# An attention and gated-MLP kernel on one core: blocks 3 to 8 in pairs with seven products of sums, and all work behind the first block in one written order

## The chip, the cores and the metric

The kernel runs on one core of one Trainium2 chip. The metric is device time of one execution in microseconds, the median of several runs. The engines are named as in the profile: PE (TensorE; PEld is its weight load), DVE (VectorE), ACT (ScalarE), POOL (GpSimd), SP (SyncE, which here only issues DMA).

## The reference

Attention of q over keys and values that were averaged over groups of eight positions (B, H, S, D = 8, 8, 576, 64), then an RMS norm and a gated MLP over all 4608 tokens (512 to 1536 to 512), all in float32:

```python
k_p = k.reshape(B, H, Sp, 8, D).mean(axis=3); v_p = ...      # 72 pooled keys
attn = softmax(scale * q @ k_p^T)                              # over 72 keys
x = (attn @ v_p)                     # to (4608, 512)
xn = x / sqrt(mean(x * x) + 1e-6) * rms_g
g, val = xn @ w_gate, xn @ w_val
out = (g * sigmoid(g) * val) @ w_out
```

The MLP weights come as float64 words.

## The kernel before, in words

Every float32 operand of a large matrix product is split into a high part (rounded to fp32r) and a low part (the rest); a product is the sum of three matmuls, high by high, low by high, high by low. Tokens are worked in nine blocks of 512 (`NB`), numbered 0 to 8; the attention is worked in eight batches of 576 tokens, so a block takes tokens from one or two batches. The hidden size of 1536 is cut into 12 pieces f of 128 gate and 128 value columns, written 0 to b in the orders.

For a block i and a piece f: `mm1(i, f, 0)` and `mm1(i, f, 1)` (12 matmuls each over four chunks c of 128 inputs, line 490) fill one PSUM bank with the gate and one with the value; `gate` (ACT, Silu, L497) and `val` (DVE, L502) make the activation; `act_hi` (ACT, L506) and `act_lo` (DVE, L510) split it; `mm2` (L521) adds 12 matmuls into four PSUM banks that hold the block's output until the last f, when it is copied and stored (L527, L528).

The attention of a batch goes by four pairs of heads: pooled keys and values (DVE, L228, L239), scores (`s_heads`, PE, L282), softmax with maximum, subtraction, exponent, sum, and the scaling on POOL (L291 to L299), a transpose on DVE and twelve small DMA copies that place the blocks (`s_turn`, L304, L309), the product with the values (`s_av`, PE, L343), copies, squares (ACT) and their sum (POOL, L384). After four pairs `s_sums` and `s_rms` give the norm's factor: PE sums over partitions (L399), ACT takes the root, DVE the reciprocal (L402), and DVE scales the tokens (L404).

Block 0, the attention of batches 0 and 1 and the conversion of the weights follow an order written out by hand (`ORDER`, one letter a step). The rest is laid out by loops: for each block the split of its tokens (`split_x`, L462, L463), then for each f the two halves of the first layer, the second layer of the f before, and between them, by slots, the attention steps of later batches. Each engine runs its instructions in the order in which they stand.

## Time and profile before

| | |
|---|---|
| median of 3 runs | 1048.86 us (1048.38 to 1048.91) |
| the profiled execution | 1049.04 us, its span 1047.3 us |
| PE busy | 1026.6 us, 98% of the span |
| DVE, ACT, POOL busy | 506.3, 416.6, 115.9 us |
| DMA | 65.44 MB, mean 62 GB/s |

The span runs from the first to the last instruction. Busy times are those of one engine alone, so they overlap. A group of instructions is one line of the program on one engine with one shape: its busy time, the mean of one, then the idle time of the engine just before them and who ended it. The chain that ended last is followed back from the last instruction; it is 88% PE, 5% DVE.

### The profile page before, as it was taken

Reading aid. Unit: us, or ns where it says so; the run is one execution under the profiler, and the core shown is the slowest. Engines: PE = TensorE matmul, PEld = TensorE weight load, DVE = VectorE, ACT = ScalarE, POOL = GpSimd, SP = SyncE. Lnnn points to the kernel's source line nnn. Section 1 sums busy time; section 2 is a strip of 40 time slices with the busy share of each in tenths; the row PEclk is TensorE's granted clock in tenths of the full one; section 3 lists DMA queues with packets and bytes.
Section 4 is the critical chain, followed back from the end, with each engine's and each line's share of the span. In section 5 each row is a group of like instructions: output and inputs, shape, how many; then the busy total and the mean of one; then the engine's idle time right before and its main releaser. Section 6 shows DMA issues by size and latency. Waiting matters only on the chain.

```text
span 1047.3 us, 13134 instructions
## 1 busy us (share of the span) xinstructions
PE 1026.6 (98%) x4994; PEld 816.2 (78%) x4994; DVE 506.3 (48%) x857; ACT 416.6 (40%) x771; POOL 115.9 (11%) x108
## 2 busy tenths in 40 slices
PE   7899998999999999999999999999999999999998
PEld 6677776777877777777877787778777888888886
DVE  6799985635455446344653455445452431122112
ACT  5767664433443345333533354335342431121111
POOL 2313430111001100111001101110011000000000
PEclk8599999999999999999999999999999999999999
DMA  9445412222022201221122103210210010001001
GB/s 292 133 163 177 170 62 72 74 76 74 25 73 73 58 25 50 77 66 36 43 75 54 57 3 108 55 53 12 88 36 14 1 41 1 1 1 41 1 1 40
DMA packets 38702, 65.44 MB, mean 62 GB/s; under 512 B 6384, under 2 KB 20208, under 8 KB 37360
## 3 DMA queue, kind: packets, MB, share of 16 engines
q1 hardware_dynamic: 38640, 64.61, 20.3%
q8 instruction: 39, 0.64, 0.3%
q14 instruction: 23, 0.19, 0.1%
HBM read 47.19 MB, written 9.44 MB: 54 GB/s over the span
## 4 chain that ended last, share of the span: by engine, by line
PE 88%; DVE 5%; DMA 2%; ACT 2%; issue 1%; SPq 0%; ACTq 0%
PE psg L490 53%; PE po L521 27%; PE pss L282 4%; PE psx L343 3%; DVE wt L140 1%; DMA wx<-w 1%; DVE wt L144 1%; DMA main<-kT 1%; DVE wt L136 1%; ACT prob L260 1%; PE psr L412 1%; DVE w L162 0%; PE pst L323 0%; PE psb L436 0%; DMA q<-qT 0%
## 5 line engine op out<-in xcount | busy, mean ns | idle before, releaser
L490 PE MATMUL psg<-xh,w 128*128 128x512 f32 x1728 | 541.3, 395 | 2.9 <-ACT xh L462 2.9
L490 PEld LDWEIGHTS psg<-xh,w 128*128 128x128 f32 x1728 | 322.3, 189 | 82.9 <-ACT xraw L350 3.4
L490 PE MATMUL psg<-xl,w 128*128 128x512 f32 x864 | 338.2, 392 | 0.0
L521 PE MATMUL po<-w,hh 128*128 128x512 f32 x864 | 223.3, 395 | 0.0
L502 DVE TENSOR_TENSOR act<-act,psg 128x512 f32<-128x512 f32 x108 | 73.6, 682 | 288.1 <-PE psg L490 254.5
L521 PEld LDWEIGHTS po<-w,hh 128*128 128x128 f32 x864 | 162.6, 188 | 37.7
L490 PEld LDWEIGHTS psg<-xl,w 128*128 128x128 f32 x864 | 162.6, 188 | 35.5 <-DVE xl L463 0.7
L506 ACT CAST hh<-act 128x512 fp32r<-128x512 f32 x108 | 67.1, 622 | 212.5 <-DVE act L502 212.4
L497 ACT ACTIVATE act<-psg 128x512 f32<-128x512 f32 x108 | 64.5, 597 | 204.8 <-PE psg L490 202.6
L521 PE MATMUL po<-w,hl 128*128 128x512 f32 x432 | 122.4, 395 | 0.4 <-DVE hl L510 0.4
L521 PEld LDWEIGHTS po<-w,hl 128*128 128x128 f32 x432 | 79.5, 188 | 20.3 <-DVE act L502 2.0
L510 DVE TENSOR_TENSOR hl<-act,hh 128x512 fp32r<-128x512 f32 x102 | 70.0, 686 | 40.9 <-ACT hh L506 38.5
L299 POOL TENSOR_TENSOR prob<-prob,sm 128x360 f32<-128x360 f32 x48 | 38.7, 826 | 446.2 <-DVE sm L297 257.9
L497 ACT ACT_TABLE_LOAD x40 | 51.3, 1283 | 47.8 <-PE psg L490 26.6
L291 DVE TENSOR_REDUCE mx<-pss 128x5 f32<-128x360 f32 x48 | 23.4, 528 | 49.8 <-PE pss L282 49.6
L304 DVE STREAM_TRANSPOSE sq<-prob 128x960 f32<-128x960 f32 x24 | 28.3, 1179 | 38.8 <-POOL prob L299 34.6
L384 POOL TENSOR_TENSOR acc<-acc,sq 128x576 f32<-128x576 f32 x21 | 30.7, 1461 | 146.4 <-ACT sq L378 146.4
L239 DVE TENSOR_REDUCE pv<-v 72x128 f32<-72x1024 f32 x28 | 34.0, 1214 | 22.8 <-PE psx L343 21.5
L282 PEld LDWEIGHTS pss<-pk,q 64*128 64x128 f32 x560 | 34.5, 193 | 12.0 <-issue 8.9
L282 PE MATMUL pss<-pk,q 64*128 64x72 f32 x560 | 38.6, 283 | 1.8 <-DVE own L329 0.9
L294 ACT ACTIVATE prob<-prob 128x360 f32<-128x360 f32 x48 | 23.1, 505 | 31.9 <-DVE prob L293 31.8
L343 PE MATMUL psx<-pt,pv 72*64 72x256 f32 (+2 forms) x224 | 35.4, 429 | 0.0
(90 smaller groups left out, 701.2 us busy)
## 6 DMA issues: line engine op xcount, KB each, us to landing
wx<-w SPq DMA_DIRECT2D x10, 1024.0 KB
v<-vN SPq DMA_DIRECT2D x32, 288.0 KB
out<-o SPq DMA_DIRECT2D x36, 256.0 KB
wx<-w SPq DMA_DIRECT2D x16, 512.0 KB
k<-kT SPq DMA_DIRECT2D x28, 288.0 KB
q<-qT SPq DMA_DIRECT2D x28, 288.0 KB
pt<-sq SPq DMA_DIRECT2D x96, 40.0 KB
pt<-sq SPq DMA_DIRECT2D x96, 32.0 KB
```

Of the source, the lines that this page charges most:

```text
L239: nc.vector.tensor_reduce(pv, s["v"], AX.X, ALU.add)
L282: nc.tensor.matmul(s["ps", h][:, t * SP:(t + 1) * SP], s["q"][r, o:o + P], s["pk"][r, :], start=True, stop=True)
L299: nc.gpsimd.tensor_tensor(pr, pr, sm[:, :, None].broadcast_to(shape), ALU.mult)
L304: nc.vector.transpose(sq.rearrange("p b g j -> p g b j"), prob.rearrange("p g (b j) -> p g b j", b=3))
L343: nc.tensor.matmul(ps[r, :n], s["pv"][:, r], s["pt"][:, h, tok], start=True, stop=True)
L384: nc.gpsimd.tensor_add(acc[b], acc[b], st[b, p]["sq"])
L490: nc.tensor.matmul(ps[:, :NB], w[:, c, cols], x[c], start=(j == 0), stop=(j == len(todo) - 1))
L497: nc.scalar.activation(t, ps[:, :NB], AF.Silu)
L502: nc.vector.tensor_mul(t, t, ps[:, :NB])
L506: nc.scalar.copy(a, st["act"])
L510: eng.tensor_sub(l, st["act"], hh[i, f].bitcast(F32))
L521: nc.tensor.matmul(po[i][t], x[i, f][:, t * P:(t + 1) * P], w, start=(f == 0 and k == 0), stop=(f == NF - 1 and k == 2))
```

## The change

The loops behind block 0 are replaced by a second written order, `LATER`, of 2279 steps with names of two letters and digits (batch, pair, head or block, f, product). Each engine again takes its own steps in that order. The tokens of block 1 are split (`t0` to `t3`) ahead of the last second-layer step of block 0 (`ob`).

Blocks 1 and 2 keep the old first layer (`mg`, `me`). Blocks 3 and 4, 5 and 6, 7 and 8 form pairs. For a pair, the tokens of the two blocks and the two halves of the 512 inputs form a 2 by 2 matrix A of parts (A11, A12 of the first block, A21, A22 of the second), gate and value columns and the two halves of the inputs a 2 by 2 matrix B; the four products of the first layer come from seven products of parts and of sums of parts (Strassen's scheme in Winograd's form):

```python
PRODUCTS = (("A11", "B11"), ("S2", "T2"), ("A12", "B21"), ("S3", "T3"), ("A22", "T4"), ("S1", "T1"), ("S4", "B22"))
```

The sums S of tokens are made by DVE (`p_sum`, step `ys`), split by ACT and DVE (`yh`, `yl`). The sums T of weights are made once, during blocks 1 and 2, on POOL (`wt`, `wf`), split by ACT and POOL (`wh`, `wl`) and stored to DRAM (`ws`); the weights' own blocks are stored as well (`wd`). Each product then loads its weights (256 KB) from DRAM into one of eight buffers (`rl`), in order on SP's queue. A product is six matmuls:

```diff
+    def product(i, f, k):
+        if k in (0, 4):
+            st["X"] = bank(2, f"px{i}_{f}_{k}")
+        elif k in (1, 3, 5):
+            st["Y"] = bank(3, f"py{i}_{f}_{k}")
+        ps = st["Y"] if k in (1, 3, 5, 6) else st["X"]
+        w, x = ring[i, f, k], XP[i, PRODUCTS[k][0]]
+        more = k in (2, 6)
+        todo = [(c, h) for c in range(2) for h in ((0, 0), (1, 0), (0, 1))]
+        for j, (c, (a, b)) in enumerate(todo):
+            nc.tensor.matmul(ps[:, :NB], w[:, a, c, :], x[:, b, c, :],
+                             start=j == 0 and not more, stop=j == len(todo) - 1, skip_group_check=more)
```

Between the products DVE and ACT take the sums out of the two banks:

```diff
+            cp=lambda i, f: S_.copy(later(i, f), st["X"]),
+            u2=lambda i, f: V.tensor_add(u2(i), later(i, f), st["Y"]),
+            sa=lambda i, f: S_.activation(new_act(i, f), st["X"], AF.Silu),
+            u3=lambda i, f: V.tensor_add(u3(i), u2(i), st["Y"]),
+            c2=lambda i, f: V.tensor_sub(later(i, f), u3(i), st["X"]),
+            sw=lambda i, f: S_.activation(later(i, f), later(i, f), AF.Silu),
+            v2=lambda i, f: V.tensor_add(u3(i), u3(i), st["Y"]),
+            v1=lambda i, f: V.tensor_add(u2(i), u2(i), st["Y"]),
+            va=lambda i, f: V.tensor_mul(st["act"], st["act"], u2(i)),
+            vb=lambda i, f: V.tensor_mul(later(i, f), later(i, f), u3(i))))
```

The first block's second layer runs in two halves (`mp`) among the products of the next f; the activations of the second block are kept (`later`) and its second layer (`mo`) runs by itself behind the pair, with the outputs of the first block copied (`ev`) and stored (`st`) ahead of it.

The scaling of a batch is now four instructions for each half of its tokens, with the gain in it, so that the split of later blocks has no factor; the scores are laid out so that a copy of the transposed blocks is contiguous:

```diff
-        x = xraw[b][:, :, tok]
-        nc.vector.tensor_mul(x, x, r[:, None, :].broadcast_to([P, NC, n]))
+    def l_scale(b, u):
+        r, tok = half(b, u)
+        for c in range(NC):
+            x = xraw[b][:, c, tok]
+            nc.vector.scalar_tensor_tensor(x, x, gcol[:, c:c + 1], r, ALU.mult, ALU.mult)
...
-                    t[32 * i:32 * i + n, :, o:o + w],
-                    sq[32 * a:32 * a + n, i].rearrange("p (h t) j -> p h (t j)", h=2)[:, :, :w])
+                nc.sync.dma_start(t[32 * i:32 * i + n, o // 16:(o + w) // 16, :],
+                                  sq[32 * a:32 * a + n, i, :w // 16, :])
```

Of the order, the end of block 2 with the start of the first pair, a step of the first pair, the end of that pair, and a step of the last pair (steps of all engines; `mo`, `mp`, `rm`, `sc`, `av`, `pr` are PE's):

```diff
+ mo2a vl2b wf93 wh91 sh4 wl93 hi2b sl4 wl91 lo2b ws93 rm40:0 ws91 rm41:1 rt40 rl300 rl301 rl302
+rl303 rt41 rl304 rc40 rl305 sc51:01 wh94 rl306 wl94 rl310 wh92 lv52 rc41 wl92 ws94 lk52 ws92 wtb rs41 wfb0 rs40 wfb1
+wfb2 wfb3 ys33 yh30 yh32 yl30 whb3 yh33 wlb3 ys34 pr300 yh31 wsb3 rl311 yl33 whb2 yh34 wlb2 ys35 cp30 wsb2 whb1 wlb1
+yl34 yh35 wsb1 yl35 pr301 whb4 wlb4 ys36 rl312 wta wsb4 u230 yh36 yl31 wfa0 wfa1 wha1 yl36 pr302 wfa2 wha3 wla3 yl32
+mp2b0 rl313 sa30 wfa3 wsa3 wla1 pr303
...
+pr310 rl320 v130 va30 sq50 pr311 rl321 cp31 sm510 hi30 ev22 nm510 pr312 rl322 lo30
+st22 ev23 u231 st23 mp300 sa31 rl323 tr51 sc52:01 dm51 pr313 mx521 sb521 mx520 pr314 ex521 u331 sb520 pr315 c231
+ex520 sm521 sw31 mp301 v231 nm521 sm520 pr316 vb31
...
+pr3b6 lk71 vb3b nm701 av630:1 rl510 v13b av631:0 va3b xc630 tr70 hi3b xc631 lo3b
+dm70 xd63 mo3b hi40 pv71 lo40 sq63 pk71 jn63 mo40 hi41 ev30 ev31 ev32 ev33 lo41 sh6 mo41 sl6 hi42 lo42
...
+pr720 rl730
+v171 va71 pr721 rl731 cp72 hi71 pr722 lo71 rl732 u272 mp710 rl733 sa72 pr723 pr724 rl734 u372 pr725 rl735 c272 sw72
+mp711 rl736 v272 vb72 pr726
```

More of the change, by code (lines that the diff above doesn't have):

```diff
@@ L448, in body, with tokens @@
     hh, hl, po = {}, {}, {}
-    def split_x(i):
-        XH[i] = [sb1.tile([P, NB], F32R, tag=f"xh{c}", name=f"xh{i}_{c}") for c in range(NC)]
-        XL[i] = [sb1.tile([P, NB], F32R, tag=f"xl{c}", name=f"xl{i}_{c}") for c in range(NC)]
-        parts, t = [], i * NB
-        while t < (i + 1) * NB:
+    tails = {}
+    def tokens(t, n):
+        parts, end = [], t + n
+        while t < end:
             b, o = divmod(t, S)
-            n = min(S - o, (i + 1) * NB - t)
-            parts.append((xraw[b], o, n, t - i * NB))
+            n = min(S - o, end - t)
+            x, first = tails.get(b, ((xraw[b][:, :2], xraw[b][:, 2:]), 0))
+            parts.append((x, b, o - first, n))
@@ new lines, in place, with w_sum, w_sumhi @@
+    def place(f, name):
+        r, c = {**BLOCKS, **SUMS}[name]
+        return st["whole", f][:, 2 * r:2 * r + 2, c * P:(c + 1) * P]
+    def w_sum(f, k):
+        y, a, b = (("T1", "T3", "T1"), ("T3", "B22", "T3"), ("T2", "B22", "T1"), ("T4", "T2", "B21"))[k]
+        nc.gpsimd.tensor_sub(place(f, y), place(f, a), place(f, b))
+    def w_sumhi(f, k):
+        if f < AHEAD:
+            y = sb2.tile([P, 2, 2, P], F32R, tag="out", name=f"wt{f}_{k}")
+        else:
+            turn = st["turn"] = 1 - st.get("turn", 0)
+            y = room()[:, 1, :].rearrange("p (s h c n) -> p s h c n", s=2, h=2, c=2)[:, turn].bitcast(F32R)
+        st["parts", f, k] = y
+        nc.scalar.copy(y[:, 0], place(f, f"T{k}"))
@@ new lines, in w_sumlo, with w_store, at @@
+    def w_sumlo(f, k):
+        y = st["parts", f, k]
+        nc.gpsimd.tensor_sub(y[:, 1], place(f, f"T{k}"), y[:, 0].bitcast(F32))
+    def w_store(f, k):
+        x = wsums[f, k] = dram.tile([P, 2, 2, P], F32, tag=f"sum{f}_{k}", name=f"sum{f}_{k}")
+        nc.sync.dma_start(x, st["parts", f, k].bitcast(F32))
+    def at(q, k, lo, hi):
+        d = 0
+        for x, _, o, n in q:
+            if d <= lo and hi <= d + n:
+                return x[k][:, :, o + lo - d:o + hi - d]
+            d += n
@@ new lines, in p_pieces, with p_hi @@
+    def p_pieces(i, n):
+        name = XPARTS[n]
+        if name[0] == "S":
+            yield slice(0, NB), XP[name]
+            return
+        q, d = tokens((i + (name[1] == "2")) * NB, NB), 0
+        for _, _, _, m in q:
+            yield slice(d, d + m), at(q, int(name[2]) - 1, d, d + m)
+            d += m
+    def p_hi(i, n):
+        X = XP[i, XPARTS[n]] = space1(n + 1, [P, 2, 2, NB], F32R, f"xp{i}_{n}")
+        for t, x in p_pieces(i, n):
+            nc.scalar.copy(X[:, 0, :, t], x)
@@ new lines, in between, with u2, u3, later @@
+    def between(i):
+        if ("u", i) not in st:
+            st["u", i] = space1(NF - 1, [P, 4 * NB], F32, f"u{i}")
+        return st["u", i]
+    def u2(i):
+        return between(i)[:, :NB]
+    def u3(i):
+        return between(i)[:, NB:2 * NB]
+    def later(i, f):
+        if ("hb", i, f // 4) not in st:
+            st["hb", i, f // 4] = space1((9, 8, 10)[f // 4], [P, 4, NB], F32, f"hb{i}_{f}")
+        return st["hb", i, f // 4][:, f % 4, :]
+    def new_act(i, f):
+        t = st["act"] = sb1.tile([P, NB], F32, tag="act", name=f"act{i}_{f}")
+        return t
@@ L481, in mm1 @@
     def mm1(i, f, which):
-        ps = st["psg", which] = bank(1, f"psg{i}_{f}_{which}")
+        ps = st["psg", which] = bank(2 + which, f"psg{i}_{f}_{which}")
         cols = slice(which * P, (which + 1) * P)
@@ new lines, in o_copy @@
+    def o_copy(i, t):
+        name = f"o{i}_{t}"
+        if i == NBLK - 1:
+            o = sb1.tile([P, DM], F32, tag=f"xh{t}", name=name)
+        elif i >= FIRST and not second(i):
+            if ("o", i) not in st:
+                st["o", i] = space1(0, [P, NB // P, DM], F32, f"o{i}")
+            o = st["o", i][:, t, :]
+        else:
+            o = sb2.tile([P, DM], F32, tag="out", name=name)
+        st["o", i, t] = o
+        (nc.scalar.copy if t % 2 else nc.vector.tensor_copy)(o, po[i][t])
@@ L569, in first_phase, with o_store, run @@
+    def o_store(i, t):
+        nc.sync.dma_start(out[i * NB + t * P:i * NB + (t + 1) * P, :], st["o", i, t])
+    def run(order, n, steps):
+        for step in order.split():
+            step, _, banks = step.partition(":")
+            given[:] = [int(x) for x in banks]
+            steps[step[:n]](*(int(x, 36) for x in step[n:]))
+            assert not given, step
     def first_phase():
@@ L596, in body @@
         first_phase()
[L597 to L631 removed]
+        later_phase()
 def kernel(q, k, v, moe_w_gate, moe_w_val, moe_w_out, moe_rms_g):
```

425 lines of the change are left out of this document (284 added, 141 removed).

## The prediction

> **What bounds the kernel now.** I read the page's busy times, then the windows by stage (columns: stretch, its length, then for PE, PEld, DVE, ACT, POOL busy us and instructions; granted clock, DMA share, GB/s), then the chain.
>
> ```profile
> span 1047.3 us, 13134 instructions
> PE 1026.6 (98%) x4994; PEld 816.2 (78%) x4994; DVE 506.3 (48%) x857; ACT 416.6 (40%) x771; POOL 115.9 (11%) x108
> ```
>
> ```profile
> 0.00:57.00 57.00, 47.82 (x279) 36.33 (x280) 42.33 (x90) 38.72 (x146) 14.52 (x19) 0.67 0.62 195
> 57.00:176.00 119.00, 114.02 (x565) 89.70 (x563) 103.41 (x133) 72.30 (x149) 37.05 (x23) 1.00 0.38 128
> 176.00:184.00 8.00, 5.39 (x15) 3.90 (x16) 5.29 (x11) 4.26 (x10) 0.00 (x0) 0.79 0.72 216
> 184.00:510.00 326.00, 325.82 (x1631) 258.00 (x1630) 160.91 (x290) 132.61 (x203) 33.54 (x35) 1.00 0.20 56
> 510.00:843.00 333.00, 333.00 (x1634) 263.96 (x1634) 153.41 (x276) 133.31 (x207) 30.83 (x31) 1.00 0.16 47
> 400.00:510.80 110.80, 110.80 (x550) 87.77 (x549) 52.97 (x97) 45.31 (x71) 10.78 (x11) 1.00 0.19 54
> 843.00:942.00 99.00, 99.00 (x435) 81.25 (x434) 21.66 (x34) 18.40 (x30) 0.00 (x0) 1.00 0.03 11
> ```
>
> From 184 us on TensorE (PE) is never idle (325.82 of 326, 333.00 of 333), at full clock. So from there the time is the number of matmuls by their pace, and other engines count only where they make PE wait. Block 7 (843 to 942) has no attention beside it and takes 99.0 us; a block with one batch of attention takes 110.8. A batch thus costs PE 11.8 us (2.95 for each of four head pairs), and DVE 52.97 - 21.66 = 31.3. The pace of a matmul, from the chain:
>
> ```profile
> 925.42 5.47 PE psg L490 x24
> 930.89 2.77 PE po L521 x12
> 933.66 5.47 PE psg L490 x24
> ```
>
> 36 matmuls take 933.66 - 925.42 = 8.24 us, 0.229 each. The only loss behind the first block is at the start of block 1, in the timeline of PE:
>
> ```profile
> 175.08 0.63 PE L521 MATMUL po<-w,hh 128*128 128x512 f32 x2
> 178.61 0.73 PE L490 MATMUL psg<-xh,w 128*128 128x512 f32 x2 [2.91 <-ACT xh L462]
> ...
> 180.72 1.06 PE L490 MATMUL psg<-xh,w 128*128 128x512 f32 x2
> 181.58 0.63 PE L490 MATMUL psg<-xl,w 128*128 128x512 f32 x1
> ```
>
> PE idles 2.91 us for the split of block 1, and its matmuls then come every 0.43 us (180.72, 181.58: two each) until 183.5. That is half pace; the window 176 to 184 shows the clock, 0.79 on average.
>
> **Part 1, seven products: what goes.** A pair of blocks computes, for each of the 12 column pairs f, 7 products of 6 matmuls (42) where two blocks took 2 x 24 = 48. The second layer stays at 24. 6 x 12 x 3 pairs = 216 matmuls fewer: 216 x 0.229 = **-49.4 us**. The attention's own matmuls stay, as many as before.
>
> **Part 2, start of block 1.** Its split (t0 to t3) now stands ahead of the last second-layer step of block 0 and is hidden by it. The 2.91 us of idle go, and half of a slow stretch of about 3.4 us: **-4.6**. If that cover failed, these 4.6 would stay.
>
> **Part 3, the products' chain.** Per f PE now runs 42 + 12 matmuls, 12.36 us. DVE has u2, u3, c2, v2, v1, va, vb, lo; ACT has cp, sa, sw, hi. Nearest rows by form and the timeline around one release:
>
> ```profile
> L502 DVE TENSOR_TENSOR act<-act,psg 128x512 f32<-128x512 f32 x108 | 73.6, 682 | 288.1 <-PE psg L490 254.5 <-issue 33.6
> L510 DVE TENSOR_TENSOR hl<-act,hh 128x512 fp32r<-128x512 f32 x102 | 70.0, 686 | 40.9 <-ACT hh L506 38.5 <-PE po L521 2.4
> L506 ACT CAST hh<-act 128x512 fp32r<-128x512 f32 x108 | 67.1, 622 | 212.5 <-DVE act L502 212.4
> L497 ACT ACTIVATE act<-psg 128x512 f32<-128x512 f32 x108 | 64.5, 597 | 204.8 <-PE psg L490 202.6 <-POOL hl L510 1.3 <-DVE hl L510 0.6
> L497 ACT ACT_TABLE_LOAD x40 | 51.3, 1283 | 47.8 <-PE psg L490 26.6 <-DVE hl L510 21.0
> ```
>
> ```profile
> 185.95 0.39 PE L490 MATMUL psg<-xl,w 128*128 128x512 f32 x1
> 186.44 0.69 DVE L502 TENSOR_TENSOR act<-act,psg 128x512 f32<-128x512 f32 x1 [0.45 <-PE psg L490]
> 187.17 0.62 ACT L506 CAST hh<-act 128x512 fp32r<-128x512 f32 x1 [3.04 <-DVE act L502]
> ```
>
> DVE 8 x 0.68 = 5.5 us, ACT 2.4. The last matmul starts at 185.95, so its place ends at 186.18; DVE begins 0.26 later, and the next engine 0.04 after DVE ends. Products write banks X, Y in turn, and a bank read by DVE must be free one group (6 x 0.229 = 1.37 us) later: 0.26 + 0.68 + 0.04 = 0.98. cp needs 0.26 + 0.60 + 0.04 = 0.90; sa with a table load has two groups, 2.74, for 2.2. So a pure pair step makes no wait, with 0.4 us to spare; cover gone, each late 0.5 us costs 0.5. In the first pair DVE has two batches besides (2 x 31.3), the last parts (some 12) and 12 x 5.5: 141 us of PE's 12 x 12.36 + 8 x 2.95 = 172, or 82%, in one fixed order. The attention's instructions:
>
> ```profile
> L291 DVE TENSOR_REDUCE mx<-pss 128x5 f32<-128x360 f32 x48 | 23.4, 528 | 49.8 <-PE pss L282 49.6
> L293 DVE TENSOR_TENSOR prob<-pss,mx 128x360 f32<-128x360 f32 x48 | 23.7, 522 | 0.0
> L296 DVE TENSOR_REDUCE sm<-prob 128x5 f32<-128x360 f32 x48 | 23.0, 521 | 0.3
> L298 DVE RECIPROCAL sm<-sm 128x5 f32<-128x5 f32 x48 | 8.0, 187 | 0.1
> L304 DVE STREAM_TRANSPOSE sq<-prob 128x960 f32<-128x960 f32 x24 | 28.3, 1179 | 38.8 <-POOL prob L299 34.6 <-DMA pt<-sq 4.2
> ```
>
> I followed one full step by hand, f = 1, from the start of pr310: v1 ends at 0.94, va 1.6, sm (0.52 and two small ones) 2.5, an output copy 3.2, lo 3.9, u2 4.6 (its bank is wanted at 7.1), tr 5.8; scores end at 7.1; mx, sb, mx to 8.95, u3 9.6 (wanted 9.84), sb 10.2, c2 10.9, sm 11.8, v2 12.5 (wanted 12.6). It fits by 0.1 us. So the waits lie between nothing and half a us in each of the 24 steps of the two pairs with attention (12); I take **+4**, nearer the low end, as that step fits.
>
> **Part 4, start of the first pair.** Block 4 needs batch 4, whose scaling is the last work of stage two (blocks 1 and 2). PE's order there is mo2a, rm40, rm41, sc51, pr300, pr301, pr302. On DVE stand between rm41 and pr300: rc40, rc41, rs41, rs40 (four instructions each), ys33, yl30. Nearest rows:
>
> ```profile
> L401 ACT ACTIVATE acc<-psr,eps 128x288 f32<-128x288 f32 x12 | 6.0, 500 | 7.9 <-PE psr L399 7.9
> L402 DVE RECIPROCAL acc<-acc 128x288 f32<-128x288 f32 x12 | 23.4, 1952 | 13.1 <-ACT acc L401 13.0
> L463 DVE SCALAR_TENSOR_TENSOR xl<-xraw,gcol,xh 128x320 fp32r<-128x320 f32 x8 | 4.3, 543 | 2.3 <-ACT xh L462 2.3
> L463 DVE SCALAR_TENSOR_TENSOR xl<-xraw,gcol,xh 128x256 fp32r<-128x256 f32 x8 | 3.4, 478 | 2.3 <-ACT xh L462 2.3
> L162 DVE TENSOR_TENSOR w<-wt,w 128x1024 fp32r<-128x1024 f32 x6 | 7.3, 1215 | 0.0
> ```
>
> 288 columns lie between 0.478 and 0.543: 0.51. These two rows leave some 0.2 that no column pays for (0.543 less 320 times 0.065 / 64). A sum over 1024 is 1.2, and 0.15 to 0.2 more for each further piece: ys 1.5 in three pieces, yl of a block 1.4 in two, of a sum 1.25. Root 0.5 + 2 x 1.95 + 8 x 0.51 + 1.5 + 1.4 = 11.4; PE has sc51 alone beside it (half of a head pair's 2.95, 1.5): it waits 9.9. pr301 needs S2: ys34, yl33, ys35, yl34 = 5.5 against one product of 1.37: 4.1. pr302 needs A12, behind yl35, ys36, u230: 4.8 against 1.37: 3.4. **+17.4**. Ends: 12, if the two later waits are mostly hidden by slower products; 25, if rm40 comes late as well, behind a join and copies.
>
> The eight rs run while POOL makes the last weight sums. In the first phase such instructions got long:
>
> ```profile
> L140 DVE SCALAR_TENSOR_TENSOR wt<-wx,wt x26: 652/1200/3405, 28.2 to 157.6; 128x512 uint32<-128x512 uint32 x16, 128x1024 uint32<-128x1024 uint32 x10
> L249 DVE TENSOR_SCALAR mx<-mx x16: 169/171/1708, 10.1 to 138.4; 128x5 f32<-128x5 f32 x16
> ```
>
> ```profile
> L162 POOL TENSOR_TENSOR w<-wt,w 128x1024 fp32r<-128x1024 f32 x4 | 10.0, 2503 | 21.4 <-ACT w L158 21.4
> L299 POOL TENSOR_TENSOR prob<-prob,sm 128x360 f32<-128x360 f32 x48 | 38.7, 826 | 446.2 <-DVE sm L297 257.9 <-DVE sm L298 188.3
> ```
>
> L249 goes from 0.17 to 1.71 us, L140 (two forms) to 3.4. Eight rs, each 0 to 1 us longer: 0 to 8, taken **+3**. [...]
>
> **Part 5, end of each pair.** After the last product come v1, va, hi, lo ahead of the last second-layer step: 0.26 + 0.68 + 0.69 + 0.62 + 0.69 = 3.0 us, 3.5 where tr70 or two copies come between. PE has av (1.5) beside it in two pairs, nothing in the third: 2.05 + 2.05 + 3.0. Then lo of the second block waits until `hl` is read (the tenth of twelve matmuls), and ev30 follows it: 0.26 + 0.69 + 0.68 less 2 x 0.23 = 1.1, three times. **+10.5** (6 to 14). The parts of pairs two and three are made beside the second block's twelve second-layer steps: 12 x 2.77 = 33 us of PE; DVE has 12 lo (8.2), rc (3.9), rs (4.1), ys (4.5), yl (7) and copies (1.4), 29: nothing. Without that cover it would be Part 4 again, twice.
>
> **Part 6, clock.** A 2.9 us idle cost a half-clock stretch of 3.4, that is 1.7 us. Such follow Part 4 once and Part 5 up to three times: 0 to 6.8, taken **+3.4**.
>
> **Part 7, weight sums and DMA.** 12 x 2.5 (1024 columns on POOL) and 96 of 256 columns at 0.5 to 0.83 (L299 has 360) are 78 to 110 us of POOL in stage two, whose PE time is 2 x 99 + 3 x 11.8 = 233, with norms and joins 30 more; hidden. DVE has 2 x 21.66 + 3 x 31.3 = 137, ACT less. SP issues:
>
> ```profile
> L528 SPq DMA_DIRECT2D out<-o x36: 332/344/436, 174.4 to 1044.2; - x36
> L309 SPq DMA_DIRECT2D pt<-sq x288: 585/608/1464, 195.5 to 795.5; - x144
> ```
>
> 252 loads, 48 stores and 24 block copies at some 0.34 us, and twelve 0.6 for each head pair: in the first pair 84 x 0.34 + 8 x 7.2 = 86 of 172 us. A load is issued seven products (11 us) ahead, as its buffer comes free; a load held behind the transposes' copies on SP still has 7. The loads ask for 7 x 0.262 MB per 12.36 us, 149 GB/s; the windows above moved 195 at a share of 0.62 and 128 at 0.38, so about half of the engines. Nothing, from both.
>
> **Sum.** Against the profiled 1049.04 (span 1047.3 and 1.7 around it): -49.4 - 4.6 + 4 + 17.4 + 3 + 10.5 + 3.4 = -15.7, so 1033.3; the median shown is 0.2 lower: **1033**.
>
> **Rivals.** *The gain arrives nearly whole (14%).* If the first pair's parts were ready early and the clock stayed, Parts 3, 4, 6 shrink to 12: 1049 - 54 + 12 + 6 = 1013. For it: PE's order was full before. Against: the DVE sum of Part 4. *Attention comes late in stage two (16%).* POOL's norms queue behind weight sums, and each of 12 head pairs' av waits a us: 1045. For: L299 stood alone before; against: about 20 us lie between scores and av. *Slower: the clock gate oscillates in the pairs (8%).* From 0 to 57 us PE was busy 84% and got a clock of 0.67; from 57 to 176, 96% and 1.00. If DVE's 82% load leaves PE idle by more than those 4% in the first two pairs, one half-clock stretch in each of 24 steps costs 24 x 1.7 = 41: 1074. Ten stretches decide. [...] *Slower too: loads late (4%).* At 120 GB/s a step lasts 15.3 us, +3 x 36: 1139; below 143 the gain is gone. For it: rows of 1 KB, which no row here prices; against: the shares of Part 7. 58% stay for the forecast, with 1020 to 1042 as its own range.
>
> **Numbers.** What the rivals and bounds leave: 1010 to 1050. No change means within 0.2% (2.1 us), what a measurement here can tell. Faster: 58 + 14 + 11 of the late case = 83%; same 3 (late case); slower 8 + 4 + 2 = 14%.
>
> **What would show it.** PE matmuls 216 fewer at 0.229; a start of block 1 without idle; some 10 us without matmul ahead of pr300, then 4 and 3, released by DVE; three waits of 3 to 4 us at pair ends; f-steps of 12.4 us in the last pair. Wrong, if the gap ahead of pr300 is short, if steps of the last pair are longer than 12.4, if PE waits for DMA, or if the clock falls within pairs.

## The result and the profile after

The changed kernel takes 1073.49 us (median of 4 runs, 1072.06 to 1075.04; the profiled one is the slowest of them), the kernel before beside it 1048.66: a ratio of 1.0237, 95% interval 1.0219 to 1.0255. It is slower by 24.8 us, where the prediction had 1033 and a range of 1010 to 1050. A run that took over 1.5% longer than the fastest of its kernel is left out of the times below, which concerns one run, of e2.

The page of the profiled execution after: span, busy times, granted clock in 40 slices, DMA.

```profile
span 1072.7 us, 13968 instructions
PE 1006.1 (94%) x4778; PEld 781.9 (73%) x4778; DVE 676.3 (63%) x1090; ACT 458.3 (43%) x849; POOL 230.2 (21%) x216
PEclk7599999899999999599999999999999999999999
DMA packets 113781, 156.74 MB, mean 146 GB/s; under 512 B 11568, under 2 KB 70704, under 8 KB 112432
```

The 216 matmuls are gone (4994 to 4778), but PE, busy 98% of the span before, is busy 94% now. The windows by stage of the changed kernel (stretch, length, then PE, PEld, DVE, ACT, POOL busy us and instructions; granted clock, DMA share, GB/s):

```profile
175.00:427.70 252.70, 240.00 (x1242) 184.40 (x1240) 155.92 (x269) 130.20 (x215) 117.33 (x122) 0.99 0.55 165
427.70:455.00 27.30, 11.10 (x24) 7.05 (x25) 26.63 (x32) 11.82 (x20) 20.15 (x15) 0.52 0.52 163
455.00:634.70 179.70, 170.63 (x835) 129.81 (x833) 123.10 (x218) 79.34 (x117) 23.76 (x25) 0.99 0.61 175
634.70:679.50 44.80, 40.87 (x181) 32.83 (x182) 31.11 (x50) 18.26 (x28) 1.41 (x1) 0.92 0.23 64
679.50:839.90 160.40, 157.80 (x709) 122.54 (x707) 85.46 (x140) 46.70 (x76) 8.04 (x9) 1.00 0.54 158
878.50:1030.70 152.20, 148.42 (x638) 119.27 (x636) 68.30 (x101) 31.95 (x53) 0.00 (x0) 1.00 0.47 138
```

Rows one to six are blocks 1 and 2, the start of the first pair, the rest of its first layer, the second layer of its second block (block 4), and the first layers of pairs two and three. PE stands still 12.7 us in the first, 16.2 in the second, 9 in the third, 4 in the fourth. In the second DVE is full (26.63 of 27.30) and POOL is busy for 20.15. Before, PE was busy for 325.82 of the 326 us from 184 to 510.

The waits of PE in the changed kernel (what waited, for what: us in all, times, longest):

```profile
PE px L774 <- DVE xp L748: 13.6, 2, 9.0
PE po L863 <- DVE hl L849: 11.9, 7, 3.0
PE po L863 <- DVE o L877: 8.8, 4, 3.9
PE pss L399 <- DMA q<-qT: 6.4, 2, 4.7
```

These are the parts of the first pair, the low parts and output copies, and q. The prediction had the first at about this size (9.9 and 3.4). Of the low parts, 6.7 stand at the pair ends (7.1 forecast), of the output copies 6.5 (3.3 forecast). The wait for q it had not.

To compare kernels I use one measure: each step of PE has a length when nothing holds it (a first- or second-layer step 12 x 0.229, a product 6 x 0.229, scores 1.6, av 0.70 for a half, a total 0.26), and what a step takes beyond that until the next one starts is its **excess**. The kernel before has -1.6 by this measure from block 1 on, as the lengths for attention are a little long. Summed by stage, the profiled run has:

```text
stage (start us)         blocks   first     block   pair two  block   pair    block   sum
                         1, 2     pair      4       first     6       three   8
                         175      427.7     634.7   679.5     839.9   878.5   1030.7
after                    16.9     35.8      7.0     6.1       2.4     6.6     1.8     76.6
predicted                 0       24.4 (start 20.4, products' chain 4), ends 10.5, clock 3.4   38.3
```

The start of the first pair (scores sc51 to the first second-layer part of block 2's last step) has 24.8, of which 2.3 stand in the first column, as sc51 begins at 423.8; some 11 lie behind it, in the pair's interior; the three pair ends, spread over the last five columns and the end of the second, have 16.9.

### The profile page after: what moved, and what is told of

The parts are those of the page before. It is cut to its first block, busy times and chain, and to the rows that moved or that the text cites. A ratio compares the mean times of both kernels' runs of the same rounds, so it can differ in the third digit from the quotient of the medians.

```text
span 1072.7 us, 13968 instructions
## 1 busy us (share of the span) xinstructions
PE 1006.1 (94%) x4778; PEld 781.9 (73%) x4778; DVE 676.3 (63%) x1090; ACT 458.3 (43%) x849; POOL 230.2 (21%) x216
## 4 chain that ended last, share of the span: by engine, by line
PE 72%; DVE 10%; DMA 8%; SPq 4%; issue 2%; ACT 2%; POOL 0%; DVEq 0%; ACTq 0%
PE po L863 24%; PE py L774 16%; PE psg L822 12%; PE px L774 11%; DMA v<-vN 4%; PE pss L399 3%; SPq L443 3%; PE psx L480 3%; DMA sum<-room 1%; DMA q<-qT 1%; DVE wt L267 1%; PE pst L456 1%; DVE wt L271 1%; DMA main<-kT 1%; DVE hl L849 1%
## 5 line engine op out<-in xcount | busy, mean ns | idle before, releaser
L774 PE MATMUL py<-xp,wp 128*128 128x512 f32 x864 | 228.2, 399 | 6.2 <-DVE u L921 2.4
L774 PEld LDWEIGHTS py<-xp,wp 128*128 128x128 f32 x864 | 162.1, 190 | 50.6 <-DVE u L921 3.7
L774 PE MATMUL px<-xp,wp 128*128 128x512 f32 x648 | 173.1, 402 | 15.7 <-DVE xp L748 13.6
L822 PE MATMUL psg<-xh,w 128*128 128x512 f32 x576 | 183.9, 401 | 0.0
L774 PEld LDWEIGHTS px<-xp,wp 128*128 128x128 f32 x648 | 123.0, 191 | 48.1 <-DVE xp L748 14.8
L822 PEld LDWEIGHTS psg<-xh,w 128*128 128x128 f32 x576 | 106.4, 189 | 29.9 <-issue 2.4
L822 PE MATMUL psg<-xl,w 128*128 128x512 f32 x288 | 113.5, 396 | 0.0
L849 DVE TENSOR_TENSOR hl<-act,hh 128x512 fp32r<-128x512 f32 x66 | 49.3, 748 | 31.5 <-ACT hh L844 30.6
L921 DVE TENSOR_TENSOR u<-u,py 128x512 f32<-128x512 f32 x36 | 24.6, 684 | 66.6 <-PE py L774 66.2
L822 PEld LDWEIGHTS psg<-xl,w 128*128 128x128 f32 x288 | 54.4, 189 | 12.9
L356 DVE TENSOR_REDUCE pv<-v 72x128 f32<-72x1024 f32 x28 | 33.7, 1204 | 28.3 <-DMA v<-vN 28.3
L849 DVE TENSOR_TENSOR hl<-hb,hh 128x512 fp32r<-128x512 f32 x36 | 24.7, 686 | 42.1 <-ACT hh L844 36.5
```

Of the source, the lines that this page charges most:

```text
L356: nc.vector.tensor_reduce(pv, s["v"], AX.X, ALU.add)
L774: nc.tensor.matmul(ps[:, :NB], w[:, a, c, :], x[:, b, c, :], start=j == 0 and not more, stop=j == len(todo) - 1, skip_group_check=more)
L822: nc.tensor.matmul(ps[:, :NB], w[:, c, cols], x[c], start=(j == 0), stop=(j == len(todo) - 1))
L849: eng.tensor_sub(l, act_in(i, f), hh[i, f].bitcast(F32))
L921: u3=lambda i, f: V.tensor_add(u3(i), u2(i), st["Y"]),
```

## The experiments

**One part alone: Part 2 in the kernel before (e3_before_split).** The split stands ahead of the last second-layer step of block 0; nothing else is changed.

```diff
-Fa B11:1 H10 ia o9 H11 gb:2 La eb:3 Gb oa Fb ib jb ob k20 v20
+Fa B11:1 H10 ia o9 H11 gb:2 La eb:3 Gb oa Fb ib jb t0 t1 t2 t3 ob k20 v20
...
         first_phase()
-        split_x(1)
```

> The kernel before with Part 2 alone: the split of block 1's first tile stands ahead of the last second-layer product of block 0, as in the changed kernel; nothing else is changed. If the prediction's Part 2 holds by itself: 4.6 us less, 1044 us. If the gain is taken back at once by the next thing that is late (in the changed kernel the first attention of block 2 waited 4.7 us for q a little later): 1048 to 1049 us.

Measured: 1051.82 us against 1047.81, ratio 1.0040 (1.0024 to 1.0056): 4 us slower where 4.6 less were due. Its timelines of SP, DVE and PE behind the split:

```profile
176.46 3.78 SPq L530 DMA_DIRECT2D out<-o  x4
180.28 0.46 SPq L200 DMA_DIRECT2D k<-kT  x1
184.19 0.35 SPq L208 DMA_DIRECT2D q<-qT  x1
```

```profile
172.54 3.29 DVE L465 SCALAR_TENSOR_TENSOR xl<-xraw,gcol,xh 128x64 fp32r<-128x64 f32 x8
175.75 0.69 DVE L529 COPY o<-po 128x512 f32<-128x512 f32 x1
183.41 0.75 DVE L228 TENSOR_REDUCE pk<-k 128x72 f32<-128x576 f32 x1 [4.06 <-DMA k<-kT]
```

```profile
187.68 1.73 PE L282 MATMUL pss<-pk,q 64*128 64x72 f32 x13 [6.18 <-DMA q<-qT]
```

The split's 3.29 us stand on DVE ahead of block 0's output copy. SP issues these in the written order: the four stores wait for the copies (176.46, before 174.36), k for the stores (180.28), the reduce of k begins at 183.41, q is issued behind that reduce (184.19), as both use one buffer, and the scores wait for q 6.18 us. Before, the wait for the split ran beside that chain and hid it: there the scores start at 186.52, with a wait for q of 0.18. So the scores come 1.2 us later than before; the other part of the 4 us stands behind them, where the granted clock is at half from 184.7 to 194.9 (before, from 180.1 to 183.5). The step failed in what is queued behind it: the split moved onto DVE ahead of the copies, and with them stores and loads.

**The same with block 2's first loads early (e3b_before_early).**

```diff
-Fa B11:1 H10 ia o9 H11 gb:2 La eb:3 Gb oa Fb ib jb t0 t1 t2 t3 ob k20 v20
+Fa k20 v20 B11:1 H10 ia o9 H11 K20 V20 gb:2 La eb:3 Gb oa Fb ib jb t0 t1 t2 t3 ob
...
-        steps.append(lambda: (pool_k(first), pool_v(first)))
+        steps.append(lambda: None)
```

> The kernel before with Part 2 as in the run that was slower by 0.4 per cent, and beside it the loads and reduces of block 2's first heads (k, its reduce, q, v and its reduce) issued while block 0 still multiplies, so that they stand ahead of block 0's four stores on the queue and of the split on VectorE. If that run was slow because q, which is behind k's reduce, came 6.2 us late behind the split and the stores: 4 to 5 us less than before, 1043 to 1045 us. If the split itself costs what its earlier place gains: 1048 to 1052 us.

Measured: 1046.72 us against 1049.12, 0.9975 (0.9960 to 0.9990). 2.4 us of the 4.6 come; the chain was the reason, though not all of the gain returns. The profiled run, one of the slowest of the twelve (1050.18), has a wait of 2.54 us for the weights of attention (av) at 201.9 that the kernel before has not, and half clock for 6.8 us behind it.

**The same in the changed kernel (e11_q_early).** There q waits in this way, with two block copies on the queue ahead of it:

```profile
179.39 1.40 SPq L661 DMA_DIRECT2D blocks<-w  x2
180.89 1.33 SPq L327 DMA_DIRECT2D q<-qT  x1
```

```profile
188.43 0.92 PE L399 MATMUL pss<-pk,q 64*128 64x72 f32 x6 [4.69 <-DMA q<-qT]
```

```diff
-Fa B11:1 H10 ia o9 H11 gb:2 La eb:3 Gb oa Fb ib jb k20 v20 t0 t1 t2 t3 ob
+Fa k20 v20 B11:1 H10 ia o9 H11 K20 q20 V20 gb:2 La eb:3 Gb oa Fb ib jb t0 t1 t2 t3 ob
...
-wd0 mg10 kt1 pk20 wt0 pv20 lq20 lv21 wf00 me10 gt10 wf01 wh01 wf02 wh03 wl03 mg11 wf03 vl10 ws03 wl01 hi10 lo10 ws01
+wd0 mg10 kt1 wt0 lv21 wf00 me10 gt10 wf01 wh01 wf02 wh03 wl03 mg11 wf03 vl10 ws03 wl01 hi10 lo10 ws01
```

> The changed kernel with the loads and reduces of block 2's first heads issued while block 0 still multiplies, and nothing else moved. The wait for q at 183.7 us (4.7 us, and half clock for 6.8 us behind it, 6.9 in all) goes. If nothing else stands right behind it: 1066 to 1068 us. If the sums and the attention of block 2, which now come earlier against the same loads, take it back: 1070 to 1074 us.

Measured: 1075.86 us, 1.0248 (1.0216 to 1.0279), no gain. The wait at 183.7 is gone, and the third scores of block 2 wait for their q 2.89 us at 215.4, with half clock behind it (4.8 us of excess in the next steps). So in this run 4.8 of the 6.9 us come back at the next load that is late.

**Leaving out streams.** e1 loads the product weights once for each pair, e2 makes the sums and block copies once, e10 does both; the outputs are then not the reference's.

```diff
+        if f:
+            ring[i, f, k] = ring[i, 0, k]
+            return
```

```diff
-            src = wblocks[f][c, :, :, 2 * r:2 * r + 2, :]
+            src = wblocks[0][c, :, :, 2 * r:2 * r + 2, :]
...
-            src = wsums[f, int(name[1])]
+            src = wsums[0, int(name[1])]
```

(and in e2 and e10 the steps wd, wt, wf, wh, wl, ws of all f but 0 are taken from the order)

> The changed kernel without the stream of product weights: for each pair the 28 KB-per-partition set of the seven products is loaded for the first part of the hidden layer only and used again for the other eleven (their output is then not the reference's; all products, waits and other loads stay). After is 1073.5 us, of which 77 us stand above the sum of its stages without waits. Theory T1 (v, k and q arrive late because the weight stream fills the queue and the chip's transfers; the engines in their fixed order stand behind them): the late landings of v go back from a median of 5.2 us to about 3 us, the first pair's interior and the pair ends lose most of what they have above the base, 10 to 15 us in all, so 1058 to 1063 us. Theory T2 (the waits come from VectorE and ScalarE, which have too much to do in a fixed order at the start and end of a pair): 1071 to 1074 us, the waits stand where they stood.

> The changed kernel in which the weight sums and the copies of the blocks into DRAM are made for the first part of the hidden layer only and used for all twelve (output not the reference's; the loads of the product weights stay). It leaves out some 11/12 of GpSimd's work for the sums, and of their loads and stores. Theory T3 (the sums are not free: their loads hold back q and v of blocks 1 and 2, and GpSimd's work stretches VectorE's at the start of the first pair): the 16.9 us above base in blocks 1 and 2 fall by 5 to 8, the start of the first pair's 24.8 by 3 to 5, so 1061 to 1066 us. Theory T4 (the sums lie beside other work, as the prediction's Part 7 had it): 1071 to 1074 us.

> The changed kernel with both streams left out: the weight sums and block copies are made for the first hidden part only, and each pair loads the first part's product weights only (output not the reference's). Alone, the loads left out gave 4.7 us and the sums some 13. If they cost by different ways (sums by holding VectorE, loads by making k, q and v late): both together 17 to 20, so 1054 to 1057 us. If both are one thing, the transfers: no more than the larger, 1060 to 1063 us. What then remains above the kernel before is order and chain alone.

Measured: e1 1068.76 (1.0192, 1.0169 to 1.0215), e2 1060.65 (three runs, 1055.5 to 1063.9; 1.0109, 1.0072 to 1.0145), e10 1055.47 (1.0065, 1.0045 to 1.0084). Neither T1 nor T2 for e1: about 5 us, a third to a half of what I expected. For e2 T4 is out, and T3's range begins just above; but T3 looked for most of it in blocks 1 and 2, and it comes at the start of the first pair (table below). The sums cost some 13, and both together 18.0, so within the spread of these runs they add. So Part 7's "nothing, from both" was worth 18 us. The profile used here is that of e10, which leaves out both.

Where the sums cost shows in the eight scalings (rs, 128x288) at the start of the first pair; count, then shortest, median, longest ns. After:

```profile
L556 DVE SCALAR_TENSOR_TENSOR xraw<-xraw,gcol,acc x8: 502/972/2375, 427.6 to 434.3; 128x288 f32<-128x288 f32 x8
```

and e10, POOL idle:

```profile
L546 DVE SCALAR_TENSOR_TENSOR xraw<-xraw,gcol,acc x8: 512/512/519, 424.6 to 427.7; 128x288 f32<-128x288 f32 x8
```

It is the sums and not the stream of loads: in e1, which has the sums and leaves out the loads, the eight take 506/973/2375. The excess at this start falls from 24.8 to 16.0 in e10. The timeline of the changed kernel around it, and one of block 1:

```profile
214.22 2.41 POOL L674 TENSOR_TENSOR wsum<-w 128x1024 f32<-128x1024 f32 x1
214.99 1.18 DVE L435 STREAM_TRANSPOSE sq<-prob 128x960 f32<-128x960 f32 x1
216.10 1.08 DVE L849 TENSOR_TENSOR hl<-act,hh 128x512 fp32r<-128x512 f32 x1
...
427.30 2.36 POOL L674 TENSOR_TENSOR room<-w 128x1024 f32<-128x1024 f32 x1
427.59 6.81 DVE L556 SCALAR_TENSOR_TENSOR xraw<-xraw,gcol,acc 128x288 f32<-128x288 f32 x7
429.73 3.51 POOL L683 TENSOR_TENSOR room<-room 128x256 f32<-128x256 f32 x4
```

The low part (L849, 0.69 us elsewhere) begins at 216.10 and ends at 217.18: 0.55 after POOL's addition has ended at 214.22 + 2.41 = 216.63. The first scaling begins at 427.59 and, 2.38 long, ends 0.31 after the addition that ended at 429.66. The transpose (L435) beside the same kind of addition keeps its 1.18.

**How VectorE is held (e12_quarters, e13_order_quarters).** The addition of 1024 columns is cut into four; e13 is the same in the best order (below).

```diff
-        nc.gpsimd.tensor_add(t, W1[f][:, 0].bitcast(F32), W1[f][:, 1].bitcast(F32))
+        for c in range(NC):
+            nc.gpsimd.tensor_add(t[:, c], W1[f][:, 0, c].bitcast(F32), W1[f][:, 1, c].bitcast(F32))
```

> The changed kernel with the first addition of each weight sum (1024 columns on GpSimd, 2.4 to 2.5 us, twelve times) cut into four of 256 columns (0.75 us each); the same sums, order and loads. In the changed kernel VectorE instructions on SBUF operands that begin while a GpSimd instruction runs end only after that one has ended (2.38 us in place of 0.51 for the first scaling at 427.6, behind an addition of 2.36). Theory H (VectorE is held until the one GpSimd instruction ends, then goes next): no such instruction is held longer than about 1.0 us more, the longest scaling falls from 2.38 to about 1.0, and the start of the first pair gets 1 to 3 us shorter: 1069 to 1073 us. Theory B (both share a path and are slowed alike as long as both have work): the scalings keep their sum of 7.8 us, the longest stays near 2, 1073 to 1075 us.

> The second new order (1035.0 us) with the same cut of the additions into four. Under H, the instructions of VectorE that still meet such an addition are held 0.7 us at most in place of 2.4; few are left that do, so 1032 to 1036 us. Under B: 1035 to 1037 us.

The scalings in e12:

```profile
L556 DVE SCALAR_TENSOR_TENSOR xraw<-xraw,gcol,acc x8: 634/972/982, 433.1 to 439.0; 128x288 f32<-128x288 f32 x8
```

The longest falls from 2.38 to 0.98, as H says, with additions of 0.77 to 0.84 us (means of L675) in place of 2.40 to 2.50 (L674). But seven of eight now take 0.97, about one of POOL's instructions each (the four from 432.64 take 3.42), so their sum hardly moves (7.8 to 7.4). The time was missed by both theories: 1079.80 (1.0275, 1.0248 to 1.0303). POOL's additions take 38.0 us in place of 29.7, and the second total of block 4's norm starts at 428.5, not at 423.1. But PE does not wait there: the time was lost before, mostly to half clock that lies behind waits at 318.2 and 362.1 and in the changed kernel does not, though it has waits there too (2.62 and 1.91 us against 2.21 and 1.49). Whether the cut brings that or chance was not separated. e13: 1037.23 (0.9879, 0.9857 to 0.9900), above both ranges and like e9 below.

**Order alone, place by place.** The steps, their instructions and transfers stay; only the order is rewritten, in one stretch each.

e4, the start of the first pair (two lines of the order on each side):

```diff
-gt2b wf92 jn43 wh93 mo2a vl2b wf93 wh91 sh4 wl93 hi2b sl4 wl91 lo2b ws93 rm40:0 ws91 rm41:1 rt40 rl300 rl301 rl302
-rl303 rt41 rl304 rc40 rl305 sc51:01 wh94 rl306 wl94 rl310 wh92 lv52 rc41 wl92 ws94 lk52 ws92 wtb rs41 wfb0 rs40 wfb1
...
+ws92 me2b gt2b vl2b rm40:0 rt40 rc40 rm41:1 wfb0 wfb1 rs40 yh31 yh32 mo2a hi2b ys33 ys34 sc51:01 mx510 lo2b rt41 rl300
+pr300 mp2b0 mp2b1 whb3 wlb3 yh34 yl34 ys36 sb510 rl301 pr301 wfb2 wfb3 rl302 whb2 rl303 yh33 rl304 mx511 rl305 rl306
```

> The changed kernel, with nothing but the order between the last attention scores of block 4 and the end of the first pair's first two parts written anew: the norm of block 4 is finished earlier, with the last weight sums put where they meet less of VectorE's work. T5: the 24.8 us above base at this start fall to about 10, 1055 to 1062 us. T6: they move to the next products, 1068 to 1074 us.

Measured: 1069.35 (1.0180, 1.0138 to 1.0223). That is in T6's range, and yet the start did what T5 said. The first pair's excess falls from 35.8 to 21.2, while blocks 1 and 2 have 22.3 in place of 16.9. Of these 5.4 us more, 3.6 lie ahead of the stretch that was rewritten, at waits of 2.46 and 2.92 us (2.21 and 1.49 in the changed kernel) that here have half clock behind them, and 1.7 are a new wait at 414.7. The waits did not move to the next products.

e6, inside the first pair (the lines around the scores of block 5's last heads):

```diff
-va32 xc520 pr330 xc521 xd52 hi32 sq52 lo32 pr331 rl341 cp33 jn52 pr332 rl342 u233 pv60 mp320 rl343 sa33 pr333
-sc53:01 rl344 u333 pr334 lk60 mx531 sb531 mx530 pr335 ex531 rl345 c233 sb530 mp321 rl346 v233 sw33 sm531 pr336 pk60
...
+pr332 jn51 av520:1 xc520 av521:0 xd52 xc521 sq52 jn52 pr331 sc53:01 u233 pr333 hi32 lo32 mx530 lv53 mx531 sb531 sa33
```

> The changed kernel with the order inside the first pair alone written anew (from the third part's products to the tenth's): the loads of v, k and q stand ahead of the bursts of product weights, and the reduces that wait for them behind the product chain. T5 (these loads land late because four to six product weights stand ahead of them in the queue, 7 us from issue to use where an unloaded k takes 3): the 11 us above base in the interior fall to 3 or 4, 1064 to 1068 us. T6: 1071 to 1074 us, the waits stand at the next products.

Measured: 1071.39 (1.0225, 1.0201 to 1.0250): 35.8 to 31.6 in the profiled run, about 2 us in the medians. T6 is nearer here.

e5, the pair ends, with one edit of code:

```diff
-        tag = "act" if second(i) and f % 2 else "hl"
+        tag = "act" if second(i) and f % 2 == 0 else "hl"
...
-rl505 v23b nm700 rl506 sm701 lv71 pr3b6 lk71 vb3b nm701 av630:1 rl510 v13b av631:0 va3b xc630 tr70 hi3b xc631 lo3b
-dm70 xd63 mo3b hi40 pv71 lo40 sq63 pk71 jn63 mo40 hi41 ev30 ev31 ev32 ev33 lo41 sh6 mo41 sl6 hi42 lo42 st33 st32
...
+mp3a0 mp3a1 hi3b lo3b lv71 sm700 mo3b lk71 ev30 xc631 hi40 lo40 mo40 ev31 xc630 ev32 sq63 pk71 jn63 ev33 rl503 hi41
```

> The changed kernel with the order at the three pair ends alone written anew, and in the second block of a pair the low parts beginning in the buffer of the activations. T5: the 16.9 us above base at the pair ends (8.9, 3.7 and 4.4) fall to some 7, and 1062 to 1067 us are left. T6: the waits there are the chain product, sum, gate, split, which no order shortens: 1071 to 1074 us.

Measured: 1061.92 (1.0127, 1.0107 to 1.0147), T5. The window of block 4's second layer in e5:

```profile
633.80:672.00 38.20, 38.20 (x181) 31.01 (x180) 33.41 (x54) 19.16 (x30) 2.87 (x3) 1.00 0.27 88
```

PE is busy all of 38.20 us, where after it was 40.87 of 44.80. The three ends' columns fall from 7.0, 2.4 and 1.8 to 0.4, 0.2 and 0.5. What waited was not a chain that no order shortens: the last two parts of the second-layer step before (mp3a) can run behind the last product, and lo of the second block need not wait for the buffer that mo3b still reads. Which of the two gave how much was not separated.

The excess of these profiled runs, from block 1's first matmul to the last one, parted at the steps sc51, pr303 (the end of the start) and pr3b4 (close to the first pair's end):

```text
              to sc51   start   interior   the rest   sum
after          14.6     24.3      11.6       25.6     76.1
e1, no loads   19.2     24.8       1.4       24.5     70.0
e10, neither   13.4     16.0       1.5       26.4     57.3
e12, quarters  19.0     23.4      12.1       25.0     79.6
e4, start      19.6     10.5      11.3       26.5     67.9
e6, inside     14.3     24.9       6.9       25.1     71.2
e5, ends       14.9     24.6       9.8       11.1     60.4
```

Each rewriting takes its gain where it was made, and the streams act in different places: the sums at the start, the loads inside the pair. What e1, e12 and e4 have more in the first column is mostly half clock behind waits that the changed kernel has as well (in e1 the granted clock is 0.96 from 175 to 430 us, in the changed kernel 0.98).

**The whole order (e7_all, e9_order).** The edit of the buffers as in e5, the early loads, and the whole order behind block 0 written anew, twice. In e7 one low part of block 5's sums is taken after the sum is overwritten, the work being the same. Some lines of e9's order, at the start of the first pair:

```diff
+rm40:0 rt40 wf93 lq51 lo2a wh94 wl94 mo29 rc40 rs40 gt2b ys33 ys34 rl300 rl301 rl302 nm501 rl303 rl304 rl305 rm41:1
+rt41 yh33 wh92 nm500 tr50 vl2b hi2b ws94 sc51:01 mx511 wl92 mx510 lk52 wtb wfb0 ws92 mo2a lo2b wfb1 pv51 mp2b0 whb3
+ev20 ev21 yl33 dm50 av500:1 wfb2 whb2 sb510 yh34 sb511 ex511 wlb3 wsb3 yl34 pr301 ys35 ys36 wlb2 wsb2 lv52 rl306
+whb1 wfb3 whb4 wlb4 yh35 pk52 wlb1 wta st20 rl310 wsb1 ex510 wsb4 mp2b1 rl311 rl312 pr300 cp30 pr302 yl35 rc41 u230
```

The half of block 4 that the pair needs is scaled (rs40) ahead of the other half's total, the product of S2 (pr301) goes ahead of pr300, and the last second-layer steps of block 2 (mo2a, mp2b) lie between the parts.

> The changed kernel with the same products, sums, loads and engines, its planned order alone written anew from the first product of block 1 to the end, and two small edits: the first reduce of k, the first loads of q and the first reduce of v of block 2's heads are issued while block 0 is still multiplying, and in the second block of a pair the low parts begin in the buffer of the activations and not in the one that the first block's last low part still holds. After is 1073.5 us, 77.3 us above its stages without waits: 16.9 in blocks 1 and 2, 24.8 at the start of the first pair, about 11 in its interior, 16.9 at the pair ends, the rest spread. Theory T5 (the products save what Part 1 says, and the loss is in when loads, sums and VectorE's work are issued): more than half of the 77 us goes, 1015 to 1035 us, below the kernel before. Theory T6 (the waits are work that VectorE, GpSimd and the queue have too much of; another order only moves them): 1050 to 1073 us.

Measured: e7 1051.51 (1.0023, 1.0000 to 1.0046), 22 us less than after, and yet in T6's range; the excess is 51.9. In it a low part of block 2 is held behind an addition as above (322.82 + 2.55, PE waits 2.13), and short waits bring half clock six times.

> The changed kernel with its planned order after block 0 written anew a second time, with the two edits of the first such order: the loads of block 2's first heads early, and the parity of the low parts in the second block of a pair. New against the first: no VectorE work on SBUF operands is put where a GpSimd sum runs, as far as the order allows, because the first new order showed such work standing until the sum ends (2.5 us in place of 0.7 for one low part in block 2), and short waits of TensorE are gathered, because each let the granted clock fall for 3.4 us. T5 (order is the loss): 1025 to 1042 us, faster than the kernel before at 1049. T6 (the loss is work, not order): no better than the first new order, 1046 to 1056 us.

Measured: **1035.04 us**, 0.9868 (0.9848 to 0.9888), in T5's range and 14.1 us faster than the kernel before beside it. e9's page, and its windows (blocks 1 and 2 up to pr300, which in this order stands behind pr301 and the last steps of block 2; the rest of the first pair; pair two; pair three):

```profile
span 1034.1 us, 13926 instructions
PE 998.0 (97%) x4778; PEld 774.8 (75%) x4778; DVE 672.2 (65%) x1090; ACT 456.8 (44%) x850; POOL 223.5 (22%) x216
DMA packets 113782, 156.75 MB, mean 152 GB/s; under 512 B 11568, under 2 KB 70704, under 8 KB 112432
```

```profile
179.80:433.80 254.00, 243.94 (x1251) 185.55 (x1251) 165.37 (x292) 129.30 (x221) 122.46 (x129) 0.99 0.56 171
433.80:609.50 175.70, 169.85 (x827) 127.90 (x825) 126.30 (x211) 85.83 (x127) 31.00 (x30) 1.00 0.60 182
619.60:807.60 188.00, 187.02 (x853) 146.65 (x851) 113.51 (x185) 60.88 (x95) 10.28 (x9) 1.00 0.45 136
819.90:994.00 174.10, 173.08 (x746) 139.60 (x744) 86.76 (x126) 41.11 (x66) 0.00 (x0) 1.00 0.40 125
```

The same matmuls, sums and 157 MB of transfers, 38 us less. Its excess by stage is 16.1, 10.7, 0.2, 4.2, 0.8, 3.8 and 0.5, together 36.3. The 16.1 hold most of the pair's start: 5.4 lie ahead of sc51, where the changed kernel has 14.6. The waits of VectorE for k and v, after:

```profile
DVE pv L356 <- DMA v<-vN: 28.3, 10, 5.8
DVE pk L347 <- DMA k<-kT: 11.8, 8, 4.0
```

and in e9:

```profile
DVE pk L347 <- DMA k<-kT: 3.6, 2, 2.5
```

## Why the prediction was wrong

The prediction put 38.3 us of waits against 54 saved; the changed kernel has 76.6. The step that failed most is Part 7's "Nothing, from both": the weight sums and the loads of the product weights cost 18.0 us. Part 2 had the wrong sign, and Parts 5 and 6 were sized too small. These overlap, so they do not add up to the difference. e9, with the same matmuls, sums and loads in another order, has 36.3 and takes 1035 us. That this stands next to the forecast's 38.3 and 1033 is chance: the forecast followed the changed kernel's order, and e9's waits lie elsewhere.

**Part 1** holds: 216 matmuls are gone, and the others keep their pace (0.230 us each from 1040 to 1060, before 0.229). In e9 the last matmul ends at 1030.2, in the kernel before at 1043.6, so 13.4 us earlier: -49.4 for the matmuls, -1.5 for block 1, which starts at 177.1 in place of 178.6, and +36.3 of excess make -14.6; the rest is in the lengths taken for a step.

**Part 2** failed: -4.6 became +4.0 in the kernel before with this step alone, and in the changed kernel 6.9 are lost in the wait for q and behind it, at once. I named the work that hides the split, and did not name what stands behind it on DVE and on SP. Part 2's other condition, no idle at 175, came true.

**Part 7** failed with the largest term: 0 became 18.0. I compared busy sums (POOL 110 of 233 us, SP 86 of 172, half of the DMA engines) and took what fits for free. Neither the hold on VectorE nor the latency of single loads is in such sums. The issue of q in the first pair, in the changed kernel's timelines of SP and PE:

```profile
492.86 1.49 SPq L761 DMA_DIRECT2D wp<-sum  x3
494.44 0.59 SPq L761 DMA_DIRECT2D wp<-blocks  x1
495.73 0.34 SPq L327 DMA_DIRECT2D q<-qT  x1
```

```profile
502.98 1.75 PE L399 MATMUL pss<-pk,q 64*128 64x72 f32 x20 [1.70 <-DMA q<-qT]
```

q is issued at 495.73 behind a burst of weights and used at 502.98: 7.25 us. In e3 k took 180.28 to 183.41, 3.1. The rival "loads late" spoke of throughput (120 GB/s, 1139 us); the throughput held (175 GB/s in the third window), and what was late were loads behind a burst, on which VectorE stands in fixed order. Leaving the bursts out gave 5 us in the times; in e1's profile the interior loses 10, and blocks 1 and 2 take 5 back, mostly by half clock.

**Part 4** had the right shape, in PE's timeline of the changed kernel:

```profile
427.66 0.71 PE L774 MATMUL px<-xp,wp 128*128 128x512 f32 x2 [2.12 <-DMA wp<-blocks]
437.37 2.08 PE L774 MATMUL px<-xp,wp 128*128 128x512 f32 x4 [9.00 <-DVE xp L748]
440.14 1.22 PE L774 MATMUL py<-xp,wp 128*128 128x512 f32 x2 [0.69 <-ACT xp L743]
443.25 2.07 PE L774 MATMUL py<-xp,wp 128*128 128x512 f32 x4 [1.89 <-DVE xp L748]
450.80 1.65 PE L774 MATMUL px<-xp,wp 128*128 128x512 f32 x3 [4.62 <-DVE xp L748]
```

A wait of 9.00 inside pr300 (9.9 forecast), then 0.69 and 1.89 around pr301 (4.1), then 4.62 in pr302 (3.4): 16.2 against 17.4, and 2.12 ahead of pr300 for its weights, which I had not. That the sizes come near is luck in part, as e10 without the sums shows in the same places:

```profile
430.70 2.08 PE L767 MATMUL px<-xp,wp 128*128 128x512 f32 x4 [6.84 <-DVE xp L738]
435.63 2.08 PE L767 MATMUL py<-xp,wp 128*128 128x512 f32 x4 [1.37 <-DVE xp L738]
439.91 2.07 PE L767 MATMUL px<-xp,wp 128*128 128x512 f32 x4 [1.34 <-DVE xp L738]
```

With 0.27 ahead of pr301 these are 9.8. So I put the chain alone 7.6 too long, and the sums 3.4 too short: they lengthen these waits by 6.4 where I took 3 (0 to 8). The eight scalings are 3.7 of that (7.8 us, 4.1 in e10), near the 3; the rest is in the sums and low parts of the parts behind them, for which I had taken nothing. Most of what the excess of 24.8 has beyond the waits is half clock (PE worked for 11.42 us at half clock from 428.7 on, so by my estimate 5.7 of it). That the scalings could be held at all was argued from L140 (652 to 3405 ns), rightly: the rows 502/972/2375 and 512/512/519 show it.

**Part 5**: 16.9 against 10.5 (6 to 14). I had the chain of v1, va, hi, lo at its size: its three waits are 2.05, 1.76 and 2.88. The copies' waits behind it, 1.1 each by the prediction, are 3.93, 1.64 and 0.97. Ahead of the first I missed that pv71, the reduce of a late v (issued 630.9, taken 7.7 us later), stands ahead of lo40 in DVE's order; and half clock followed (from 640.3, 6.8 us). e5 removed 11.6 us in all.

**Part 3**: 4 taken; the last pair, without attention, has 0.02 to 0.03 us a step, so the chain fits as followed by hand. The 11 us in the first pair's interior are mostly late k, v and q: e6, which issues them earlier, gives 5 of them back in its profiled run, and e1, without the weight loads ahead of them, 10.

**Part 6** was sized too small, 3.4 (0 to 6.8): half clock lay at 186.3 (6.8 us), 428.7 (27.3), 503.8 (3.4) and 640.3 (6.8), each in or behind a wait. PE worked for 4.67, 11.42, 3.40 and 5.42 us of these; at full clock that work takes half, so by my estimate some 12 us were lost, part of the excess above. I had not seen that the whole start of the pair would run at half clock. The slower rival with the same time, 1074, was an oscillation within the pairs; there the clock is 1.00 in both later pairs. Its time came true and its mechanism did not.

The rival "attention comes late in stage two" (1045, 16%) was near in place, as blocks 1 and 2 have 16.9 us where I gave it 12, but its cause is not what the runs show: 6.9 of these are the wait for q, and without the sums, in e10, some 14 remain.

What stays open: ahead of sc51, e10 keeps 13.4 of 14.6 us, of which 8.3 are the wait for q and the half clock behind it, and 4.5 another wait (2.94 at 314.6) with half clock. e9, with q early and another order, has 5.4 there; which of its changes gave how much was not separated. That DVE is held by POOL is shown by e1, e10 and e12; by what is not.

## What to carry to other kernels

A stream that fits by busy sums can still cost: price it by the longest single instruction that it can put ahead of another engine's critical step (here an addition of 2.36 us, beside which a scaling of 0.51 took 2.38), and by the loads that queue behind its bursts (here a q in use 7.25 us after its issue, where a k of e3 took 3.1). When a step is moved to an earlier place, list what then stands behind it on each engine and queue, down to the next load. And where all engines run in one fixed order, the saving of a change and the quality of its order are two measurements: here the same matmuls, sums and loads, with two small edits of code, took 1073 and 1035 us.
